# Loading the first four x tiles ahead of the key weights, in smaller pieces on two queues

## The chip, the core and the metric

The kernel runs on one core of a Trainium2 chip. Five engines take part: TensorE (PE; its weight loads are listed as PEld), VectorE (DVE), ScalarE (ACT), GpSimd (POOL) and SyncE (SP), which here does nothing but issue DMAs. ScalarE can issue DMAs too. The time is the device time of one execution in microseconds; several executions are measured and their median is given.

## What is computed

The reference mixes two blocks that read the same x (2048 tokens of 512 features, bf16) with a gate per token:

```python
g = sigmoid((x * gate_w).sum(-1, keepdims=True))
qkv = x @ wqkv                          # 32 heads of 16
pq, pk = phi(q), phi(k)                 # phi(t) = (t + 1 if t > 0 else exp(t)) + 1e-6
kv = einsum("bhsd,bhse->bhde", pk, v);  z = pk summed over s
o  = (pq @ kv) / (pq . z + 1e-6)
a  = o @ wo
b  = (silu(x @ w1) * (x @ w3)) @ w2     # 1376 hidden features
out = g * a + (1 - g) * b
```

## The kernel before, in words

The 2048 tokens are 16 tiles of 128, in four blocks of four tiles. Everything stays on chip: x is held twice, as `x_sb` (tokens on the partitions) and as `xT` (features on the partitions), and so are all weights. The feature dimension of 512 is cut into four chunks, called kc.

The work runs in three stretches. In the first, for each token tile, k is computed by four matmuls (`emit_k_mm`, line 184, one for each kc, with the tile's `xT` as the stationary operand and `wk_sb` as the moving one); ScalarE and VectorE turn it into `pk_sb` (`phi`, lines 138 to 148); GpSimd adds it to a running sum; and four matmuls accumulate XP, the product of x transposed and pk (`emit_xp`, line 204), in the PSUM tiles XP0 to XP3. The second stretch closes the attention state (q of the first block, the remainder columns of the gated block, kvT, W). The third runs through the blocks: gate and up matmuls of the feed-forward part (`emit_ffn`, lines 310 and 318), and output matmuls (`emit_out`, lines 346 to 355), with the q work of the next block between them. The output rows are stored one tile at a time (line 370).

TensorE's order is written out by hand, since its part runs under a manual schedule: it executes the matmuls in the order in which the kernel emits them and waits in that order. The loads are issued on SP's queue in the order in which they are written (lines 83 to 112), except for half of wk, which ScalarE issues at line 84, before its activation table is loaded at line 88. Each load signals its landing on one of eight semaphores that are used in turn, so that in the built program a DMA from the ninth on waits, before it is issued, for the landing of the DMA eight places earlier.

The start is special. The first block's `xT` doesn't come from a transposing load, as that of the other three blocks does (line 90), but from TensorE: `emit_xT(t)` (lines 169 to 181) makes four 128 by 128 transposes of tile t into two PSUM tiles, which VectorE (line 179) and ScalarE (line 181) copy into `xT`. These PSUM tiles are the four buffers of XP0 to XP3, used in turn, and a buffer must have been copied out before its next transpose. Before the first transposes, `emit_warm` runs nine matmuls on constants (line 165) while the first loads are under way. The first x tiles are loaded in pairs: tiles 0 and 1 by one transfer, tiles 2 and 3 by another, where each partition holds two neighbouring rows of the tensor (`x_pairs`, line 81), and the rows of the output are addressed in the same way (`out_pairs`). wk comes in two halves of two kc chunks. So TensorE transposes tiles 0 and 1, computes six k matmuls (kc 0 and 1 for tiles 0 and 1, then kc 2 and 3 for tile 0), transposes tiles 2 and 3, and finishes the other ten k matmuls:

```python
    emit_xT(0)
    emit_xT(1)
    for kc, t in ((0, 0), (1, 0), (0, 1), (1, 1), (2, 0), (3, 0)):
        emit_k_mm(k0[t], t, kc)
    emit_k_phi(k0[0], 0)
    emit_xT(2)
    emit_xT(3)
```

After that, for each tile t from 4 to 15, one XP group (four matmuls) of an earlier tile and the four k matmuls of tile t follow each other.

Of the kernel before, what the change touches and what calls it, by code (L numbers as in the profile page):

```python
# [17 lines left out]
def kernel(  # L18
# [12 lines left out]
    nc = tc.nc  # L31
    P = nc.NUM_PARTITIONS

    Bb, S, D = A_x.shape
# [4 lines left out]
    NT = S // P  # L39
    TB = 512  # L40
    NTB = S // TB
    TPB = TB // P
    FC = F // P
    FR = F - FC * P
    FM = FC * P
# [3 lines left out]
    x2d = A_x.flatten_outer_dims()  # L49
    out2d = out.flatten_outer_dims()  # L50
# [13 lines left out]
    x_sb = consts.tile([P, NT, D], BF16, name="x_sb")  # L64
    xT = consts.tile([P, KC, S], BF16, name="xT")
    wk_sb = consts.tile([P, KC, D], BF16, name="wk_sb")
    wq_sb = consts.tile([P, KC, D], BF16, name="wq_sb")
    wv_sb = consts.tile([P, KC, D], BF16, name="wv_sb")
    w1_sb = consts.tile([P, KC, FM], BF16, name="w1_sb")
    w3_sb = consts.tile([P, KC, FM], BF16, name="w3_sb")  # L70
    wr_sb = consts.tile([P, KC, NR], BF16, name="wr_sb")
    w2_sb = consts.tile([P, FC, D], BF16, name="w2_sb")
# [3 lines left out]
    wqkv_r = A_wqkv.rearrange("(kc d) n -> d kc n", d=P)  # L76
    w1_r = B_w1.rearrange("(kc d) f -> d kc f", d=P)
    w3_r = B_w3.rearrange("(kc d) f -> d kc f", d=P)
    x_r = x2d.rearrange("(t p) d -> p t d", p=P)
    dq = nc.sync  # L80
    x_pairs = x2d[0:TB, :].rearrange("(g p j) d -> g p j d", p=P, j=2)
    out_pairs = out2d[0:TB, :].rearrange("(g p j) d -> g j p d", p=P, j=2)
    dq.dma_start(out=x_sb[:, 0:2, :], in_=x_pairs[0])
    nc.scalar.dma_start(out=wk_sb[:, 0:2, :], in_=wqkv_r[:, 0:2, D : 2 * D])
    dq.dma_start(out=wk_sb[:, 2:4, :], in_=wqkv_r[:, 2:4, D : 2 * D])  # L85
    dq.dma_start(out=x_sb[:, 2:TPB, :], in_=x_pairs[1])
    pre = consts.tile([1, 1], FP32, name="pre")
    nc.scalar.activation(out=pre[:], in_=nc.const_aps.tensor(0.0, [1, 1], FP32), func=ACT.Exp)
    for tb in range(1, NTB):
        dq.dma_start(  # L90
            out=xT[:, :, tb * TB : (tb + 1) * TB], in_=x2d[tb * TB : (tb + 1) * TB, :],
            transpose=True,
        )
        dq.dma_start(
            out=x_sb[:, tb * TPB : (tb + 1) * TPB, :], in_=x_r[:, tb * TPB : (tb + 1) * TPB, :]
        )
    dq.dma_start(out=wq_sb[:], in_=wqkv_r[:, :, 0:D])
    dq.dma_start(out=wr_sb[:, :, 0:FR], in_=w1_r[:, :, FM:F])
    dq.dma_start(out=wr_sb[:, :, FR : 2 * FR], in_=w3_r[:, :, FM:F])
    with nc.allow_non_contiguous_dma(reason="one gate weight per partition and chunk"):  # L100
        dq.dma_start(
            out=wr_sb[:, :, 2 * FR : NR], in_=gate_w.rearrange("(kc d o) -> d kc o", d=P, o=1)
        )
    dq.dma_start(out=wv_sb[:], in_=wqkv_r[:, :, 2 * D : 3 * D])
    for fsl in (slice(0, FM // 2), slice(FM // 2, FM)):
        dq.dma_start(out=w1_sb[:, :, fsl], in_=w1_r[:, :, fsl])
        dq.dma_start(out=w3_sb[:, :, fsl], in_=w3_r[:, :, fsl])
    dq.dma_start(out=wo_sb[:], in_=A_wo.rearrange("(kc d) n -> d kc n", d=P))
    w2_r = B_w2[0:FM, :].rearrange("(fc f) d -> f fc d", f=P)
    for fcs in (slice(0, FC // 2), slice(FC // 2, FC)):  # L110
        dq.dma_start(out=w2_sb[:, fcs, :], in_=w2_r[:, fcs, :])
    dq.dma_start(out=w2r_sb[:FR, :], in_=B_w2[FM:F, :])

    pk_sb = consts.tile([P, NT, D], BF16, name="pk_sb")
# [5 lines left out]
        out=bm, in_=bm, pattern=[[-Dh, HPC], [0, Dh]], compare_op=ALU.is_ge, fill=0.0,  # L120
# [3 lines left out]
        out=bm, in_=bm, pattern=[[Dh, HPC], [0, Dh]], compare_op=ALU.is_ge, fill=0.0,  # L124
# [33 lines left out]
    def emit_warm(*widths):  # L158
        warm = psX.tile([P, TB], FP32, tag="XP3", name="warm")
        for n in widths:  # L160
            nc.tensor.matmul(
                warm[:, 0:n], lhsT=warm_l, rhs=warm_r[:, 0:n], start=True, stop=True
            )

    emit_warm(TB, TB, TB, TB, TB, TB, P, P, P)

    st = {}

    def emit_xT(t):
        for h in range(2):  # L170
            xTp = psX.tile([P, 2, P], BF16, tag=f"XP{(2 * t + h) % 4}", name="xTp")
            for j in range(2):
                kc = 2 * h + j
                nc.tensor.transpose(  # L174
                    out=xTp[:, j, :], in_=x_sb[:, t, kc * P : (kc + 1) * P], identity=ident[:]
                )
            xT_t = xT[:, 2 * h : 2 * h + 2, t * P : (t + 1) * P]
            if h == 0:
                nc.vector.tensor_copy(out=xT_t, in_=xTp[:])
            else:  # L180
                nc.scalar.activation(out=xT_t, in_=xTp[:], func=ACT.Copy)
# [7 lines left out]
    def emit_k_phi(k_ps, t):  # L189
        e_ins = phi(pk_sb[:, t, :], k_ps[:])  # L190
        if t == 0:
            nc.gpsimd.tensor_copy(pks[:], pk_sb[:, t, :])
        else:
            nc.gpsimd.tensor_add(pks[:], pks[:], pk_sb[:, t, :])  # L194
# [137 lines left out]
    def emit_out(tb, tt):  # L332
        t = tb * TPB + tt
        tsl = slice(tt * P, (tt + 1) * P)

        if t < NT - 1:
            parts = [(0, D, True)]
        else:
            h, q3 = D // 2, 3 * D // 4
            parts = [(0, h, True), (h, q3, False), (q3, D, True)]  # L340
        o_out = work.tile([P, D], BF16, tag="o_out", name="o_out")
        lo = 0
        for i, (a, b, store) in enumerate(parts):
            o_ps = psX.tile([P, b - a], FP32, tag=f"XP{2 + (tt + i) % 2}", name="o_ps")
            for c in range(KC):
                nc.tensor.matmul(  # L346
                    o_ps[:], lhsT=st[tb, "pqT"][:, c, tsl], rhs=W_sb[:, c, a:b],
                    start=(c == 0), stop=False,
                )
            nc.tensor.matmul(  # L350
                o_ps[:], lhsT=st[tb, "hTr"][:FR, tsl], rhs=w2r_sb[:FR, a:b],
                start=False, stop=False,
            )
            for fc in range(FC):
                nc.tensor.matmul(  # L355
                    o_ps[:], lhsT=st[tb, "hT"][:, fc, tsl], rhs=w2_sb[:, fc, a:b],
                    start=False, stop=(fc == FC - 1),
                )
            if i < 2:
                nc.scalar.activation(  # L360
                    out=o_out[:, a:b], in_=o_ps[:], func=ACT.Copy, scale=omg[:, t : t + 1]
                )
            else:
                nc.vector.tensor_scalar(
                    out=o_out[:, a:b], in0=o_ps[:], scalar1=omg[:, t : t + 1], scalar2=None,
                    op0=ALU.mult,
                )
            if store:
                rows = out_pairs[t // 2, t % 2] if t < TPB else out2d[t * P : (t + 1) * P, :]
                nc.sync.dma_start(out=rows[:, lo:b], in_=o_out[:, lo:b])  # L370
                lo = b


    k0 = [psM.tile([P, D], FP32, tag="mm", name=f"k0_{t}") for t in range(TPB)]
    emit_xT(0)
    emit_xT(1)
    for kc, t in ((0, 0), (1, 0), (0, 1), (1, 1), (2, 0), (3, 0)):
        emit_k_mm(k0[t], t, kc)
    emit_k_phi(k0[0], 0)
    emit_xT(2)  # L380
    emit_xT(3)
    for t in range(1, TPB):
        for kc in range(2 if t == 1 else 0, KC):
            emit_k_mm(k0[t], t, kc)
# [23 lines left out]
    for c in range(KC):  # L408
# [7 lines left out]
        out=kvT_sb[:], in0=kvT_ps[:],  # L416
# [26 lines left out]
    for tb in range(NTB):  # L443
        for fc in range(FC if tb == 0 else 0, FC):
            emit_ffn(tb, fc)
        nx = tb + 1
        for tt in range(TPB):
            if nx < NTB:
                emit_q(nx, tt, psX, "XP0")
                if tt % 2 == 0:  # L450
                    emit_rem(nx, tt // 2, psX, "XP1")
            emit_out(tb, tt)
            if nx < NTB:
                emit_den(nx, tt)
        if nx < NTB:
            emit_norm(nx)
# [30 lines left out]
```

## Time and profile before

| what | value |
|---|---|
| median of 4 runs | 180.09 us (180.0 to 180.59) |
| the profiled execution's own time | 180.4 us |
| its span, from the first to the last instruction | 178.7 us |
| TensorE matmul busy | 173.5 us, 97% of the span |
| VectorE, ScalarE, GpSimd busy | 118.6, 66.8, 61.4 us |
| bytes read from memory, written | 8.42 MB, 2.10 MB |
| the chain that ended last, by engine | PE 94%, DMA 3%, issue 1% |
| mean granted TensorE clock | 1.00 |

The span leaves out 1.7 us of the profiled execution's time that lie around it. The page also cuts the span into 40 slices of about 4.5 us; the first four engine rows of it give the busy share of each slice in tenths, the last two rows the share of the 16 DMA engines and what they moved:

```profile
PE   7999999999999999999999999999999999999993
DVE  1478867896998837398786375978754669776000
DMA  5999999911006010124000111240001023300011
GB/s 173 234 278 249 263 273 373 347 52 28 9 12 107 0 48 29 44 54 93 0 4 6 38 37 37 59 93 2 0 7 59 15 62 65 60 0 0 29 44 50
```

TensorE is busy in nine tenths of every slice but the first and the last; the DMA engines are busy for the first eight slices, while x and all the weights come in. A busy share says only where an engine works, not what the end waits for; that is what the chain of waits is for, which goes back from the last instruction to whatever released each step. In the timelines below, a row gives the start, the length, the engine, the line and the number of instructions merged into it, and in brackets how long the engine was idle before it and until what.

### The profile page before, as it was taken

What the parts mean: (1) busy time and instruction counts of PE and PEld (TensorE: products, weight loads), DVE (VectorE), ACT (ScalarE), POOL (GpSimd) and SP (SyncE); (2) the same over time, 40 slices, a digit from 0 to 9 for tenths busy, and PEclk for the clock granted to TensorE, in tenths of its full rate; (3) what the DMA queues carried; (4) which work ended last, traced back from release to release, by engine and by line L of the source; (5) the groups of instructions that cost most, each with busy time, mean ns of one, the idle gap of its engine ahead of it and who ended that gap; (6) DMA issues with size and microseconds to landing.
All of it is one profiled execution on the core that took longest, in us unless ns stands there. A gap on an engine that the chain in (4) does not pass through costs nothing.

```text
span 178.7 us, 2472 instructions
## 1 busy us (share of the span) xinstructions
PE 173.5 (97%) x877; PEld 84.1 (47%) x893; DVE 118.6 (66%) x205; ACT 66.8 (37%) x126; POOL 61.4 (34%) x69
## 2 busy tenths in 40 slices
PE   7999999999999999999999999999999999999993
PEld 3444444474444545444444544444545444444463
DVE  1478867896998837398786375978754669776000
ACT  4642323476533333342433333342433323341221
POOL 5186675736353323262003232620032328100000
DMA  5999999911006010124000111240001023300011
GB/s 173 234 278 249 263 273 373 347 52 28 9 12 107 0 48 29 44 54 93 0 4 6 38 37 37 59 93 2 0 7 59 15 62 65 60 0 0 29 44 50
DMA packets 29085, 14.88 MB, mean 83 GB/s; under 512 B 19632, under 2 KB 28816, under 8 KB 29072
## 3 DMA queue, kind: packets, MB, share of 16 engines
q1 hardware_dynamic: 28800, 14.46, 30.6%
q10 hardware_dynamic: 272, 0.26, 0.5%
q8 instruction: 7, 0.11, 0.3%
q14 instruction: 6, 0.05, 0.1%
HBM read 8.42 MB, written 2.10 MB: 59 GB/s over the span
## 4 chain that ended last, share of the span: by engine, by line
PE 94%; DMA 3%; issue 1%; SPq 0%; DVE 0%; DVEq 0%
PE o_ps L355 19%; PE gate_ps L310 19%; PE up_ps L318 19%; PE o_ps L346 8%; PE q_ps L217 8%; PE XP L204 8%; PE k_ps L184 6%; PE r_ps L241 3%; DMA x_sb<-in_A_x_dram 3%; PE o_ps L350 2%; PE k L184 1%; PE kvT_ps L411 0%; PE W_ps L438 0%; PE xTp L174 0%; SPq L85 0%
## 5 line engine op out<-in xcount | busy, mean ns | idle before, releaser
L310 PE MATMUL gate_ps<-xT,w_sb 128*128 128x512 bf16 x156 | 40.7, 379 | 0.2
L318 PE MATMUL up_ps<-xT,w_sb 128*128 128x512 bf16 x156 | 40.5, 379 | 0.2
L225 POOL TENSOR_TENSOR qz<-pq,z_sb 128x512 f32<-128x512 bf16 x16 | 18.5, 1164 | 60.3 <-DVE pq L145 58.4
L323 ACT ACTIVATE th<-gate_ps 128x512 bf16<-128x512 f32 x40 | 23.9, 597 | 38.1 <-PE gate_ps L310 36.6
L355 PE MATMUL o_ps<-w_sb,hT 128*128 128x512 bf16 (+2 forms) x176 | 37.3, 354 | 0.2
L325 DVE SCALAR_TENSOR_TENSOR gs<-th,gate_ps 128x512 bf16<-128x512 bf16 x40 | 27.3, 683 | 5.8 <-ACT th L323 5.6
L328 DVE TENSOR_TENSOR hT<-up_ps,gs 128x512 bf16<-128x512 f32 x40 | 27.6, 691 | 3.8
L142 DVE TENSOR_SCALAR phi_m<-phi_e 128x512 bf16<-128x512 bf16 x32 | 14.3, 447 | 19.5 <-ACT phi_e L140 19.4
L355 PEld LDWEIGHTS <-hT 128*128 128x128 bf16 x180 | 16.8, 97 | 17.9
L318 PEld LDWEIGHTS <-w_sb 128*128 128x128 bf16 x160 | 15.6, 98 | 18.9
L310 PEld LDWEIGHTS <-w_sb 128*128 128x128 bf16 x160 | 15.6, 98 | 18.6
L360 ACT ACTIVATE o_out<-o_ps,omg 128x512 bf16<-128x512 f32 (+2 forms) x17 | 11.2, 656 | 30.4 <-PE o_ps L355 30.4
L290 POOL TENSOR_TENSOR pqn<-pq,rden 128x512 bf16<-128x512 bf16 x16 | 16.6, 1058 | 14.0 <-DVE rden L283 11.7
L194 POOL TENSOR_TENSOR pks<-pks,pk_sb 128x512 f32<-128x512 f32 x15 | 17.4, 1163 | 8.1 <-DVE pk_sb L145 7.5
L228 DVE TENSOR_REDUCE den<-qz 128x32 f32<-128x512 f32 x16 | 11.0, 684 | 9.0 <-POOL qz L225 8.9
L346 PE MATMUL o_ps<-W_sb,pqT 128*128 128x512 bf16 (+2 forms) x71 | 16.5, 355 | 0.1
L217 PE MATMUL q_ps<-wq_sb,xT 128*128 128x512 bf16 x63 | 16.4, 379 | 0.1
L204 PE MATMUL XP<-pk_sb,x_sb 128*128 128x512 bf16 x62 | 16.0, 379 | 0.1
L140 ACT ACTIVATE phi_e<-k_ps 128x512 bf16<-128x512 f32 x12 | 7.2, 598 | 14.4 <-PE k_ps L184 14.4
L140 ACT ACTIVATE phi_e<-q_ps 128x512 bf16<-128x512 f32 x16 | 9.6, 597 | 7.8 <-PE q_ps L217 7.8
L184 PE MATMUL k_ps<-wk_sb,xT 128*128 128x512 bf16 x48 | 12.3, 379 | 0.1
L145 DVE SCALAR_TENSOR_TENSOR pq<-q_ps,phi_m 128x512 bf16<-128x512 f32 x16 | 11.1, 691 | 0.5
(59 smaller groups left out, 117.6 us busy)
## 6 DMA issues: line engine op xcount, KB each, us to landing
w_sb<-in_B_w_dram SPq DMA_DIRECT2D x6, 640.0 KB, 9.2
out_dram<-o_out SPq DMA_DIRECT2D x15, 128.0 KB, 1.7
x_sb<-in_A_x_dram SPq DMA_DIRECT2D x3, 512.0 KB, 4.3
x_sb<-in_A_x_dram SPq DMA_DIRECT2D x2, 256.0 KB, 3.7
wq_sb<-in_A_wqkv_dram SPq DMA_DIRECT2D x1, 512.0 KB, 6.1
wv_sb<-in_A_wqkv_dram SPq DMA_DIRECT2D x1, 512.0 KB, 6.2
wo_sb<-in_A_wo_dram SPq DMA_DIRECT2D x1, 512.0 KB, 10.6
wk_sb<-in_A_wqkv_dram ACTq DMA_DIRECT2D x1, 256.0 KB, 3.8
```

What stands on the lines that cost most here:

```text
L184: nc.tensor.matmul(k_ps[:], lhsT=xT[:, kc, t * P : (t + 1) * P], rhs=wk_sb[:, kc, :], start=(kc == 0), stop=(kc == KC - 1),)
L194: nc.gpsimd.tensor_add(pks[:], pks[:], pk_sb[:, t, :])
L204: nc.tensor.matmul(XP_ps[dc][:], lhsT=x_sb[:, t, dc * P : (dc + 1) * P], rhs=pk_sb[:, t, :], start=(t == 0), stop=(t == NT - 1),)
L217: nc.tensor.matmul(q_ps[:], lhsT=xT[:, kc, ts_tok], rhs=wq_sb[:, kc, :], start=(kc == 0), stop=(kc == KC - 1),)
L225: nc.gpsimd.tensor_tensor(out=qz[:], in0=st[tb, "pq"][:, tt, :], in1=z_sb[:], op=ALU.mult)
L310: nc.tensor.matmul(gate_ps[:], lhsT=w1_sb[:, kc, fsl], rhs=xT[:, kc, tok_sl], start=(kc == 0), stop=(kc == KC - 1),)
L318: nc.tensor.matmul(up_ps[:], lhsT=w3_sb[:, kc, fsl], rhs=xT[:, kc, tok_sl], start=(kc == 0), stop=(kc == KC - 1),)
L323: nc.scalar.activation(out=th[:], in_=gate_ps[:], func=ACT.Tanh, scale=0.5)
L325: nc.vector.scalar_tensor_tensor(out=gs[:], in0=th[:], scalar=1.0, in1=gate_ps[:], op0=ALU.add, op1=ALU.mult)
L328: nc.vector.tensor_tensor(out=st[tb, "hT"][:, fc, :], in0=up_ps[:], in1=gs[:], op=ALU.mult)
L346: nc.tensor.matmul(o_ps[:], lhsT=st[tb, "pqT"][:, c, tsl], rhs=W_sb[:, c, a:b], start=(c == 0), stop=False,)
L355: nc.tensor.matmul(o_ps[:], lhsT=st[tb, "hT"][:, fc, tsl], rhs=w2_sb[:, fc, a:b], start=False, stop=(fc == FC - 1),)
```

## The change

The first eight loads are one x tile or one kc chunk of wk each, 128 KB, instead of four loads of 256 KB. The four x tiles go first, alternating between SP's queue and ScalarE's; of the wk chunks ScalarE issues the second, SP the others. Partitions hold single rows again, so the output rows of the first block are addressed like the others. All 16 transposes stand before the first k matmul, and the order of the k matmuls among themselves is as it was. There is one 512-wide warm matmul less. Further back in SP's queue, the x tiles of blocks 2 and 3 come in one load, which stands before the last transposing load instead of partly behind it, and w1, w3 and w2 are each loaded whole instead of in halves.

```diff
-    x_pairs = x2d[0:TB, :].rearrange("(g p j) d -> g p j d", p=P, j=2)
-    out_pairs = out2d[0:TB, :].rearrange("(g p j) d -> g j p d", p=P, j=2)
-    dq.dma_start(out=x_sb[:, 0:2, :], in_=x_pairs[0])
-    nc.scalar.dma_start(out=wk_sb[:, 0:2, :], in_=wqkv_r[:, 0:2, D : 2 * D])
-    dq.dma_start(out=wk_sb[:, 2:4, :], in_=wqkv_r[:, 2:4, D : 2 * D])
-    dq.dma_start(out=x_sb[:, 2:TPB, :], in_=x_pairs[1])
+    aq = nc.scalar
+    for q, t in ((dq, 0), (aq, 1), (dq, 2), (aq, 3)):
+        q.dma_start(out=x_sb[:, t, :], in_=x_r[:, t, :])
+    for q, kc in ((dq, 0), (aq, 1), (dq, 2), (dq, 3)):
+        q.dma_start(out=wk_sb[:, kc, :], in_=wqkv_r[:, kc, D : 2 * D])
...
-        dq.dma_start(
-            out=x_sb[:, tb * TPB : (tb + 1) * TPB, :], in_=x_r[:, tb * TPB : (tb + 1) * TPB, :]
-        )
+        if tb < NTB - 1:
+            x_ts = slice(tb * TPB, (tb + 1) * TPB if tb < NTB - 2 else NT)
+            dq.dma_start(out=x_sb[:, x_ts, :], in_=x_r[:, x_ts, :])
...
-    for fsl in (slice(0, FM // 2), slice(FM // 2, FM)):
-        dq.dma_start(out=w1_sb[:, :, fsl], in_=w1_r[:, :, fsl])
-        dq.dma_start(out=w3_sb[:, :, fsl], in_=w3_r[:, :, fsl])
+    dq.dma_start(out=w1_sb[:], in_=w1_r[:, :, 0:FM])
+    dq.dma_start(out=w3_sb[:], in_=w3_r[:, :, 0:FM])
...
-    w2_r = B_w2[0:FM, :].rearrange("(fc f) d -> f fc d", f=P)
-    for fcs in (slice(0, FC // 2), slice(FC // 2, FC)):
-        dq.dma_start(out=w2_sb[:, fcs, :], in_=w2_r[:, fcs, :])
+    dq.dma_start(out=w2_sb[:], in_=B_w2[0:FM, :].rearrange("(fc f) d -> f fc d", f=P))
...
-    emit_warm(TB, TB, TB, TB, TB, TB, P, P, P)
+    emit_warm(TB, TB, TB, TB, TB, P, P, P)
...
-                rows = out_pairs[t // 2, t % 2] if t < TPB else out2d[t * P : (t + 1) * P, :]
-                nc.sync.dma_start(out=rows[:, lo:b], in_=o_out[:, lo:b])
+                nc.sync.dma_start(
+                    out=out2d[t * P : (t + 1) * P, lo:b], in_=o_out[:, lo:b]
+                )
...
-    emit_xT(0)
-    emit_xT(1)
+    for t in range(TPB):
+        emit_xT(t)
     for kc, t in ((0, 0), (1, 0), (0, 1), (1, 1), (2, 0), (3, 0)):
         emit_k_mm(k0[t], t, kc)
     emit_k_phi(k0[0], 0)
-    emit_xT(2)
-    emit_xT(3)
```

## The prediction

> **What bounds the kernel now.** I read the page's busy shares first (PE 97%), then the chain of waits, to see whether anything but PE sets the end, then TensorE's timeline in the first 10 us, since the change touches almost nothing else. The chain at the start (start us, length us, what):
>
> ```profile
> 1.72 4.60 DMA x_sb<-in_A_x_dram
> 6.32 0.05 issue
> 6.37 0.62 PE xTp L174 x8
> 6.99 2.16 PE k L184 x10
> 9.15 0.86 PE XP L204 x4
> ```
>
> The end hangs on one transfer, the second pair of x tiles: issued at 1.72, landed at 6.32. After it come eight transposes and ten k matmuls; the first XP starts at 9.15. From there on TensorE has next to no gaps (columns: length, PE, PEld, DVE, ACT, POOL busy, clock, DMA share, GB/s):
>
> ```profile
> 9.15:36.60 27.45, 27.29 (x125) 12.43 (x127) 21.43 (x35) 10.48 (x18) 19.21 (x17) 1.00 1.03 295
> 36.60:175.90 139.30, 138.51 (x712) 68.03 (x723) 93.75 (x162) 51.69 (x100) 39.13 (x40) 1.00 0.14 35
> ```
>
> So what the change does to the start of the first XP it does to the end, unless a later transfer becomes late. Everything below is a sum over 0 to 9.15. TensorE's timeline there (start, length, line, count, idle before):
>
> ```profile
> 3.35 0.39 PE L161 MATMUL warm<-const-bfloat16-1.0 128*128 128x128 bf16 x3
> 3.67 0.62 PE L174 MATMUL xTp<-ident,x_sb 128*128 128x128 bf16 x8
> 4.64 1.46 PE L184 MATMUL k<-wk_sb,xT 128*128 128x512 bf16 x6 [0.36 <-DMA wk_sb<-in_A_wqkv_dram]
> 6.37 0.62 PE L174 MATMUL xTp<-ident,x_sb 128*128 128x128 bf16 x8 [0.27 <-DMA x_sb<-in_A_x_dram]
> ```
>
> The pace is read from it: a transpose every 0.62/8 = 0.078 us, a k matmul every 2.16/10 = 0.216. Real work before 9.15 is 16 x 0.078 + 16 x 0.216 = 4.7 us; it began at 3.67, so 0.8 us are waits. They are what can be won, plus an earlier beginning.
>
> **When the bytes come.** Both versions load the same 1024 KB first, so the byte rate of before, in half microseconds, is my lower bound (GB/s is the last column; 74 in the half before 2.00):
>
> ```profile
> 2.00:2.50 0.50, 0.50 (x2) 0.15 (x1) 0.00 (x0) 0.50 (x1) 0.50 (x3) 1.00 0.83 197
> 2.50:3.00 0.50, 0.50 (x3) 0.22 (x2) 0.00 (x0) 0.26 (x2) 0.50 (x2) 1.00 0.89 311
> 3.00:3.50 0.50, 0.50 (x4) 0.22 (x3) 0.00 (x0) 0.00 (x0) 0.00 (x0) 1.00 1.09 322
> 3.50:4.00 0.50, 0.50 (x10) 0.41 (x9) 0.01 (x1) 0.00 (x0) 0.00 (x0) 1.00 0.96 279
> 4.00:4.50 0.50, 0.28 (x6) 0.20 (x3) 0.50 (x2) 0.40 (x2) 0.00 (x0) 1.00 1.13 389
> 4.50:5.00 0.50, 0.36 (x2) 0.19 (x2) 0.00 (x1) 0.26 (x1) 0.00 (x0) 1.00 1.05 388
> ```
>
> Summed, 256 KB have moved at 2.9, 512 at 3.8, 768 at 4.5, 1024 at 5.2. The upper bound is when whole transfers of that sum had landed, by issue plus time to landing:
>
> ```profile
> x_sb<-in_A_x_dram SPq DMA_DIRECT2D x1, 256.0 KB, 2.8
> wk_sb<-in_A_wqkv_dram ACTq DMA_DIRECT2D x1, 256.0 KB, 3.8
> wk_sb<-in_A_wqkv_dram SPq DMA_DIRECT2D x1, 256.0 KB, 4.0
> x_sb<-in_A_x_dram SPq DMA_DIRECT2D x1, 256.0 KB, 4.6
> xT<-in_A_x_dram SPq DMA_TRANSPOSE x1, 5.9
> ```
>
> 0.80 + 2.8 = 3.6, 0.80 + 3.8 = 4.6, 1.26 + 4.0 = 5.26, 1.72 + 4.6 = 6.32.
>
> **Part by part.** *Loads.* Issues stand 0.46 us apart on a queue (0.80, 1.26, 1.72). After: SP issues x0 at 0.80, x2 1.26, wk0 1.72, wk2 2.18, wk3 2.64; ACT issues x1 at 0.80, x3 1.26, wk1 1.72. The trace has no 128 KB load, so between the bounds I take the middle: x0 and x1 land at 3.25 (2.9 to 3.6), x2 and x3 at 4.2 (3.8 to 4.6), wk0 and wk1 at 4.9 (4.5 to 5.26). For wk3, the last, the ends are 5.2 (bytes) and 2.64 + 4.6 = 7.24 (the slowest time to landing from its later issue). The nearest row is 6.32, the same 1024 KB, then with the transposing load of xT right behind from 2.23; that starts 0.9 later now, so I take 6.1.
>
> *Warm matmuls.* One 512-wide one less, 0.43 us at the cold pace (weight loads at 1.22, 1.65, 2.08), so the warm run ends at 3.3 rather than about 3.7. x0 lands then (3.25), so nothing waits there.
>
> *ScalarE.* Two more DMA issues stand before its table load, 2 x 0.46. Its row before:
>
> ```profile
> 1.27 1.28 ACT L88 ACT_TABLE_LOAD   x1 [1.27 <-PEq L471]
> 2.57 0.20 ACT L88 ACTIVATE pre<-const-float32-0.0 1x1 f32<-1x1 f32 x1
> 4.10 0.66 ACT L181 ACTIVATE xT<-xTp 128x256 bf16<-128x256 bf16 x2 [1.33 <-PE xTp L174]
> ```
>
> The 1.33 us of idle before the first copy hides the 0.92, but hardly more: ACT is free at 3.7 and its first copy is due at about 3.7. Without that cover each microsecond of ACT delay would go onto the transposes.
>
> *Transposes.* All 16 share four PSUM buffers, so those of x2 and x3 now wait for the copies of x0 and x1: two DVE copies take 0.52, two on ACT 0.66. ACT's first two end at 3.8 + 0.66 = 4.5, DVE's earlier; with x2 and x3 landed at 4.2 the last transpose ends at about 4.5 + 0.3 = 4.85. The copies' new wait thus costs no more than about 0.1.
>
> *k matmuls.* They start at 4.9 with wk0; five (kc 0, 1 for two tiles, then kc 2) take 1.08, to 5.98; the sixth needs wk3 at 6.1; it and the ten behind it take 11 x 0.216 = 2.38, end 8.48. The first XP also needs pk of tile 0: last k matmul at 6.1 + 0.38, exponential 0.60, two DVE steps 0.28 + 0.69, with gaps about 8.1. So XP starts at **8.48 instead of 9.15: 0.67 us won.**
>
> *What is late next: xT of the second block.* The two built programs' orders show that each load waits for the landing of the one eight places earlier. Ninth was the third transposing load; ninth now is the first, behind x0. It cannot issue before 0.80 + 5 x 0.46 = 3.1, and x0 lands at 3.25; plus 5.9 that is 9.15. The fifth k tile needs it at 8.48 + 0.86 = 9.34: covered by 0.2 us. With x0 at 3.6 it is 9.5, which costs 0.16. Behind it on SP everything moves by about 1 us: xT of block 2 lands near 13.5 and is due near 16.
>
> *Merged x, w1, w3 and w2 loads.* Four SP issues fewer than split ones, no fewer bytes. The last half of w3 landed at 22.35 + 9.2 = 31.6 and the first gate matmul starts at 38.9; wholes landing even 3 us later stay hidden, since PE's 27.45 us stretch covers them. The x of blocks 2 and 3, now in one 1 MB load issued near 11.4 and due at about 22, is hidden too. The out rows change only addresses. All this: 0, up to +0.2.
>
> Sum: the profiled execution, 180.4 (span 178.7), becomes 179.7. The median of the runs is 180.09, 0.3 below that execution, so I forecast 180.09 - 0.67 = **179.4**.
>
> [...] The trace shows the clock opening inside the warm run: the narrow warm matmuls take 281 ns first and 243 on average over three, so it switched near 3.45, 2.6 us after the first matmul. After the change the warm run ends at 3.3 and transposes follow. [...] By the row the missing 0.15 us is a trifle[...], sum -0.67. [...]
>
> **The rivals.** *The last wk piece is late.* For it: eight transfers instead of four, and last in line took 4.0 to 4.6 from issue. At 4.0 wk3 lands at 6.64, XP starts at 9.02: 179.96; at 4.6 9.62: 180.56. Against: the bytes are the same and the later issues leave the queues shorter. I put it at **180.0**; it loses from a wk3 landing past 6.77.
>
> [...] The place is the 16 k matmuls. [...] **181.15**. It decides against the change from three slow k matmuls on. Against it: [...] before's four runs lie within 0.6 us.
>
> *That the change doesn't do what it says* is out: in the built order all 16 transposes stand before the k matmuls.
>
> **How the numbers follow.** Forecast 0.50 (own range 179.1 to 179.75), late wk 0.28, clock 0.22. A measurement of this kernel tells 0.3% (0.54 us) from no change, so faster means under 179.55. Faster: 0.38 of the first and 0.05 of the second, 0.43. Same: 0.12, 0.17, 0.06 = 0.35. Slower: 0.06 and 0.16, 0.22. The range 179.1 to 180.9 leaves out a little below and the upper half of the clock case.
>
> **What would show it.** Right: transposes starting at 3.3, k matmuls at 4.9 at 0.216 each, XP at 8.3 to 8.7, no new TensorE gap after. Wrong: k matmuls 0.43 apart past 5 us; an idle of over 0.5 before the sixth; a wait for xT at the fifth tile; an ACT copy starting past 4.3; any wait for w1 or w3 near 39.

## The result, and the profile after

The changed kernel takes a median of 180.85 us (180.18 to 183.0, 39 runs) against 180.25 us (179.93 to 181.11, 58 runs) for the one before on the same chip: a ratio of 1.0038, interval 1.0025 to 1.0051. It is slower by about 0.6 us, a little more than the 0.3% that a measurement can tell. Forecast was a gain of 0.67 us. The profiled execution after took 181.19 us (span 179.5), the one before 180.4 (span 178.7).

The chain of waits at the start, after (start, length, what):

```profile
1.73 3.81 DMA wk_sb<-in_A_wqkv_dram
5.58 4.35 PE k L180 x16
9.93 0.86 PE XP L200 x4
```

The chain no longer hangs on x but on a piece of wk, and the first XP starts at 9.93 instead of 9.15: 0.78 us later, which is the whole difference of the two spans. From there on TensorE has no new gap (174.7 us busy, 97% of the span). In every trace of this study but two the execution's time less the start of the first XP is 171.23 to 171.29 us: 180.4 - 9.15 before, 181.19 - 9.93 after. So all of the question lies in the first 10 us, and an execution without a trace still tells when its first XP began: the median after at 180.85 - 171.25 = 9.6, the median before at 9.0.

TensorE's timeline after, the transposes:

```profile
3.62 1.89 PE L170 MATMUL xTp<-ident,x_sb 128*128 128x128 bf16 x16 [0.17 <-DMA x_sb<-in_A_x_dram]
```

They begin at 3.62 and end at 5.51. The weight loads (PEld), one for each transpose, show the pace better than such a row, whose length has the tail of its last matmul in it. The first eight before, then the sixteen after:

```profile
3.66 0.45 PEld L174 LDWEIGHTS <-x_sb 128*128 128x128 bf16 x8
3.62 1.63 PEld L170 LDWEIGHTS <-x_sb 128*128 128x128 bf16 x16 [0.44 <-DMA x_sb<-in_A_x_dram]
```

That is 0.45/8 = 0.056 us for a transpose before and 1.63/16 = 0.102 after. The weight loads of the k matmuls after (one row for those that follow each other closely):

```profile
6.39 0.15 PEld L180 LDWEIGHTS <-xT 128*128 128x128 bf16 x1 [0.28 <-issue]
6.81 0.15 PEld L180 LDWEIGHTS <-xT 128*128 128x128 bf16 x1 [0.27 <-issue]
7.18 2.26 PEld L180 LDWEIGHTS <-xT 128*128 128x128 bf16 x11 [0.21 <-issue]
```

The first two stand 0.42 us apart, the next 0.37, and from then on it is 2.26/11 = 0.21: TensorE ran at half pace until about 7.1 us, in before's profiled execution until about 3.5. Below, "the clock opens" means this doubling of the pace. The profile's own column of the granted clock reads 1.00 in both stretches, so the moment is read from the distance between matmuls, or worked out from how long a row of them took. And the landings of the first eight loads after (queue, size, us from issue to landing):

```profile
x_sb<-in_A_x_dram SPq DMA_DIRECT2D x2, 128.0 KB, 2.8
x_sb<-in_A_x_dram ACTq DMA_DIRECT2D x2, 128.0 KB, 3.0
wk_sb<-in_A_wqkv_dram SPq DMA_DIRECT2D x3, 128.0 KB, 3.8
wk_sb<-in_A_wqkv_dram ACTq DMA_DIRECT2D x1, 128.0 KB, 4.0
```

The first x tile, 128 KB, took 2.8 us, as long as the 256 KB of before. The wk pieces issued at 1.73 landed at 5.54 and 5.73. So two things end at the same moment, the sixteenth transpose at 5.51 and the first piece of wk at 5.54.

### The profile page after: what moved, and what is told of

The parts are those of the page before. It is cut to its first block, busy times and chain, and to the rows that moved or that the text cites. A ratio compares the mean times of both kernels' runs of the same rounds, so it can differ in the third digit from the quotient of the medians.

```text
span 179.5 us, 2470 instructions
## 1 busy us (share of the span) xinstructions
PE 174.7 (97%) x876; PEld 85.0 (47%) x892; DVE 118.0 (66%) x205; ACT 66.9 (37%) x126; POOL 61.3 (34%) x69
## 4 chain that ended last, share of the span: by engine, by line
PE 95%; DMA 2%; issue 1%; SPq 0%; DVE 0%; DVEq 0%
PE o_ps L351 19%; PE gate_ps L306 19%; PE up_ps L314 19%; PE o_ps L342 8%; PE q_ps L213 8%; PE XP L200 8%; PE k_ps L180 6%; PE r_ps L237 3%; PE k L180 2%; DMA wk_sb<-in_A_wqkv_dram 2%; PE o_ps L346 2%; PE kvT_ps L406 0%; PE W_ps L433 0%; SPq L83 0%; DVE o_out L360 0%
## 5 line engine op out<-in xcount | busy, mean ns | idle before, releaser
L138 DVE TENSOR_SCALAR phi_m<-phi_e 128x512 bf16<-128x512 bf16 x32 | 13.7, 427 | 22.3 <-ACT phi_e L136 22.2
```

## The experiments

The theories: **pieces** (eight loads land later than four, and k waits for wk), **clock** (it opens late, so that transposes and the first k matmuls run at half pace), **missing warm matmul** (why the clock is late), **merged loads** (the loads further back cost something). Below, "six warms" means the six 512-wide matmuls of before in place of five. Each result stands beside runs of the kernel before on the same chip (medians 180.30 to 180.38).

### The warm matmuls

a_warm6, the changed kernel with six warms:

```diff
-    emit_warm(TB, TB, TB, TB, TB, P, P, P)
+    emit_warm(TB, TB, TB, TB, TB, TB, P, P, P)
```

> The changed kernel with the sixth wide warm matmul back, nothing else. Theory: [...] the k matmuls run 0.216 apart from the start, XP starts at 5.58 + 3.46 = 9.05 to 9.1, and the median falls by about 0.8, to 180.1. [...] the k matmuls stay slow in part and the median falls by 0.4 at most. Rival: the loss is the late landing of the first wk piece (5.53) alone: no change, 180.85.

Measured: 180.84 us (180.36 to 181.35, 22 runs) beside 180.35, ratio 1.0021 (1.0012 to 1.0029). Its chain:

```profile
3.88 1.29 PE xTp L170 x14
...
5.47 3.60 PE k L180 x16
9.07 0.86 PE XP L200 x4
```

This execution, at 180.36 the fastest of its runs, is what the theory expected: the clock opened among the transposes, by 4.9 at the latest (an estimate: the fourteen in 1.29 us are ten at 0.106 us, the 0.85/8 of w_order2's at half pace, and four at 0.056), and XP starts at 9.07. The first wk piece came early (4.8) and k waited for the transposes; the k matmuls stand 0.216 us apart, with 0.15 more before the sixth, whose wk piece, the last, landed at 6.5. But the median lost as much as without the sixth warm matmul, but one thing differs: of the 39 runs of the changed kernel six lie at 182.67 to 183.0 and none between 181.35 and 182.67; here none lies above 181.35.

b_warm5, the kernel before with five warms (the same line, one TB less):

> The kernel before with five wide warm matmuls instead of six, nothing else: the one removed matmul by itself. [...] the warm run ends at 3.3, the x tiles land at 3.6, [...] six k matmuls run at half pace between 4.64 and 7.0, which the wait for the second x pair (6.32) hides in part: median 180.3 to 180.9, more spread. Rival: the warm matmul doesn't matter, since the span was bound by the x pair at 6.32: 180.1 to 180.3.

Measured: 180.49 us (22 runs, 180.09 to 181.39 and one at 182.8), ratio 1.0008 (0.9996 to 1.0021). Its trace is of a late clock (opened near 6.5): the first eight transposes take 1.03 us, from 4.06, the six k matmuls behind them 2.02, XP starts at 9.72. The median can't be told from that of six warms.

a_warm3, the changed kernel with three 512-wide warm matmuls, shows the late opening enlarged:

```diff
-    emit_warm(TB, TB, TB, TB, TB, P, P, P)
+    emit_warm(TB, TB, TB, P, P, P)
```

> The changed kernel with three wide warm matmuls instead of five. Theory: the executions 2 us above the rest[...]: with the warm run ending at 2.4 [...] the median is 181.8 to 182.8, and the trace shows ten or more k matmuls 0.43 apart. Rival: that group has nothing to do with the warm run: the median stays at 180.9 to 181.2.

Measured: 181.92 us (181.0 to 182.82, 6 runs), ratio 1.0084 (1.0053 to 1.0115). Its weight loads of k stand 0.43 us apart up to these two rows, and 1.61/8 = 0.20 in the second:

```profile
8.36 0.15 PEld L180 LDWEIGHTS <-xT 128*128 128x128 bf16 x1 [0.27 <-issue]
8.78 1.61 PEld L180 LDWEIGHTS <-xT 128*128 128x128 bf16 x8 [0.27 <-issue]
```

The half pace lasts to about 8.8; the sixteen k matmuls take 5.04 us instead of 3.45, and XP starts at 10.89 (182.15 us). A run at 182.8 would have its XP at 182.8 - 171.25 = 11.55. With k from 5.58 on and 0.43 and 0.216 us for a matmul, that is an opening near 10.6, an estimate. Such runs came in kernels with five or three wide warms, and in none of the 21 to 28 runs each of a_warm6, a_fill, b_tail, b_k7q and w_order with w_order2, all with six, nor in any run of the kernel before (181.11 at most). That the six slow runs of the changed kernel are of this kind is inferred from their size; none of them was traced.

a_fill adds matmuls on constants between the transposes (into a bank that the k matmuls overwrite), so that TensorE works without a pause from 0.84 us on:

```diff
-    for t in range(TPB):
+    for t, n in zip(range(TPB), (256, 256, 256, TB)):
         emit_xT(t)
+        emit_fill(n)
```

> The changed kernel with the sixth warm matmul and with one matmul on constants behind each tile's transposes (256, 256, 256 and 512 wide), which do no work of the kernel. [...] all k matmuls stand 0.216 apart, XP starts near 9.05, the median is 180.0 to 180.2 and the runs at 182.7 to 183 are gone. Rival, late loads alone: the fillers add up to 0.5 us of work in front of the k matmuls but inside the wait for wk, so 180.85 to 181.2.

Measured: 180.86 us (180.51 to 181.46, 21 runs), ratio 1.0029 (1.002 to 1.0038). In its trace the clock opened only past 5.8 all the same (each four transposes took 0.43 us, the last four, from 5.80, took 0.30), k started at 6.31 and took 3.45, XP 9.77. This trace shows no earlier opening, and the fillers used up the time they were to win.

### The loads further back

b_tail, the kernel before with only the merged later loads of the change (x of blocks 2 and 3, w1, w3, w2):

```diff
+        if tb < NTB - 1:
+            x_ts = slice(tb * TPB, (tb + 1) * TPB if tb < NTB - 2 else NT)
+            dq.dma_start(out=x_sb[:, x_ts, :], in_=x_r[:, x_ts, :])
...
+    dq.dma_start(out=w1_sb[:], in_=w1_r[:, :, 0:FM])
+    dq.dma_start(out=w3_sb[:], in_=w3_r[:, :, 0:FM])
```

> The kernel before with the later loads merged as in the change (x of blocks 2 and 3 in one load, w1, w3 and w2 whole), nothing else. Both theories: no difference, 180.0 to 180.3. If the merged loads cost anything, it shows as a gap of TensorE near 22 or near 39.

Measured: 180.69 us (180.29 to 181.43, 22 runs), ratio 1.0013 (1.0002 to 1.0024). XP starts at 9.14, as before, and nothing is late between: the last VectorE instruction ends at the same 175.89. What is longer is the very end, where SP waits for the last store. The waits of SP on that store, first in b_tail:

```profile
SPq L479 <- DMA out_dram<-o_out: 1.2, 1, 1.2
```

and in b_lane, the same kernel with wq loaded in four pieces and wv in two, so that the last store again signals on the semaphore it has in the kernel before:

```profile
SPq L483 <- DMA out_dram<-o_out: 0.9, 1, 0.9
```

```diff
-    dq.dma_start(out=wq_sb[:], in_=wqkv_r[:, :, 0:D])
+    for kc in range(KC):
+        dq.dma_start(out=wq_sb[:, kc, :], in_=wqkv_r[:, kc, 0:D])
```

> b_tail with four loads more (wq in four pieces, wv in two), which come long before they are needed. In b_tail the number of DMAs is four smaller than before, so that the last output store signals on another of the eight semaphores, and the wait behind it took 1.2 us instead of 0.9. Theory that the final waits stand in the order of these semaphores: with four loads more the last store is back on the old one, the wait is 0.9 again and the median is that of before, 180.25 to 180.4. Rival, merged loads cost something themselves: 180.6 to 180.7 as in b_tail.

Measured: 180.44 us (179.88 to 181.07, 14 runs) beside 180.38, ratio 1.0004 (0.9992 to 1.0016). So merging the loads costs nothing where they are used. In the changed kernel the last wait is 0.9 as well; its loss isn't here.

### Pieces apart from the clock

To hold the clock still, the loads are put behind a delay during which TensorE is kept busy. In the first pair, b_open and a_open, twenty warm matmuls made the delay:

```diff
+    warm0 = emit_warm(psX, "XP3", *([TB] * 20))
+    for sb in (x_sb[:, 0:TPB, 0:2], wk_sb[:, :, 0:2]):
+        nc.vector.tensor_copy(out=sb, in_=warm0[:, 0:8].rearrange("p (a b) -> p a b", b=2))
```

> The kernel before [...] 20 wide matmuls on constants run first, and no load may be issued until they are done (small copies of their result into the loads' destinations hold the loads back); then 14 more warm matmuls stand where the warm run stood. All instructions of the kernel follow as before, some 9 us later. Both theories: the k matmuls run 0.216 apart in every execution. [...] This is the base for a_open.

> The changed kernel with [...] in the same way. Theory A, the loss is the clock: [...] the k matmuls start when the first wk piece lands (4.7 us after the first load's issue) and take 3.46 us, so that XP starts 8.2 to 8.3 us after the first issue, as in the kernel before (8.35): a_open is within 0.2 us of b_open. Theory B, the loss is the loads' arrival: a_open stays 0.4 to 0.7 us above b_open, as without the warm start.

Measured: 187.5 us (186.46 to 187.74, 5 runs) and 187.29 (186.57 to 188.01, 6 runs). This settled nothing: the delay is made of matmuls, and so depends on when the clock opens (20 took 5.87 us in the trace). From the first issue to XP the traces show 15.18 - 6.93 = 8.25 and 15.32 - 6.91 = 8.41.

In the second pair, b_fix and a_fix, twelve VectorE reductions (0.70 us each in both traces) make the delay, while matmuls fill most of TensorE's time up to the landing of x:

```diff
+    emit_warm(psX, "XP3", *([TB] * 28))
+    for i in range(12):
+        nc.vector.tensor_reduce(
+            out=hold[:], in_=dummy[:].rearrange("p (a b) -> p a b", b=TB // 8),
+            axis=AX.X, op=ALU.add,
+        )
```

> The kernel before behind a fixed delay: VectorE runs twelve reductions on constants (0.68 us each) before any load may be issued, while TensorE runs 28 wide warm matmuls, [...] 10 more warm matmuls stand where the warm run stood. Base for a_fix. Both theories: all k matmuls 0.216 apart[...].

> The changed kernel behind the same fixed delay, clock open. In b_open and a_open XP started 8.25 and 8.41 after the first load's issue, but the medians could not tell (the delay itself depended on the clock). Theory A, the loss is the clock alone: a_fix within 0.1 us of b_fix. Theory B, it is the loads alone: a_fix 0.5 to 0.7 above b_fix. Theory C, both: the loads cost 0.15 to 0.35 (k matmuls start at 4.73 after the first issue and take 3.46, 8.2 to 8.4, against 7.85 to 8.35 for before), the clock the rest.

Measured: b_fix 190.03 us (189.91 to 190.22, 4 runs), a_fix 190.55 (190.22 to 190.79, and one run at 192.39, 6 runs). Both issue their first load at 10.63, and behind it their k matmuls run at the open clock (ten in 2.16 us in b_fix, 0.216 each, and all sixteen in 3.61 in a_fix, against 4.35 after). The chain of b_fix:

```profile
11.55 4.28 DMA x_sb<-in_A_x_dram
...
18.66 0.86 PE XP L229 x4
```

and TensorE's timeline of a_fix:

```profile
13.51 1.40 PE L195 MATMUL xTp<-ident,x_sb 128*128 128x128 bf16 x16 [0.57 <-DMA x_sb<-in_A_x_dram]
15.54 3.61 PE L205 MATMUL k<-wk_sb,xT 128*128 128x512 bf16 x15 [0.62 <-DMA wk_sb<-in_A_wqkv_dram]
```

With the clock out of the way the change still costs 190.55 - 190.03 = 0.52 us. Transposes are done at 14.91, and TensorE then waits 0.62 us for the first piece of wk. XP starts at 19.15 instead of 18.66. The four runs of b_fix lie within 0.3 us, the 58 of the kernel before within 1.2 (four drawn from these lie within 0.6 on average). How much of that scatter is the clock's opening isn't shown, since behind the delay the loads start 10 us later too, and without it the second x pair landed anywhere from 5.78 (b_lane) to 6.62 (b_k7). The run at 192.39 has no trace; it stays unexplained.

c_fix is a_fix with the same order (x first, then wk, all transposes first) in four loads of 256 KB:

```diff
+    dq.dma_start(out=x_sb[:, 0:2, :], in_=x_pairs[0])
+    aq.dma_start(out=x_sb[:, 2:TPB, :], in_=x_pairs[1])
+    dq.dma_start(out=wk_sb[:, 0:2, :], in_=wqkv_r[:, 0:2, D : 2 * D])
+    dq.dma_start(out=wk_sb[:, 2:4, :], in_=wqkv_r[:, 2:4, D : 2 * D])
```

> a_fix with the first 1024 KB in four loads of 256 KB, in the new order (x pair 0 on SP, x pair 1 on ScalarE's queue, both wk halves on SP); wq and wv are split so that the last store signals on the same semaphore. Theory, the order costs: the first wk half lands 4.7 to 4.9 after the first issue, median 190.35 to 190.55 as a_fix. Rival, the pieces cost: it lands by 4.4, median 190.0 to 190.15 as b_fix.

Measured: 190.18 us (190.13 to 190.23, 5 runs), 0.15 behind b_fix and 0.37 ahead of a_fix. (c_fix and w_fix ran on another chip than these two; the kernel before took 180.34 there and 180.35 here.) Its chain has no wait for wk:

```profile
15.41 3.45 PE k L212 x16
18.86 0.86 PE XP L232 x4
```

The first half of wk landed at 14.80, 0.7 us before the first piece in a_fix; 0.46 of that is its place in SP's queue, second instead of third. The first x, a pair now, landed later than the single tile of a_fix, at 13.87 instead of 13.37.

w_fix keeps the pieces and the fixed delay but goes back to the old order, x0 and x1, wk, then x2 and x3, with the transposes in two groups:

```diff
-    for q, t in ((dq, 0), (aq, 1), (dq, 2), (aq, 3)):
+    for q, t in ((dq, 0), (aq, 1)):
...
+    for q, t in ((dq, 2), (dq, 3)):
+        q.dma_start(out=x_sb[:, t, :], in_=x_r[:, t, :])
```

> a_fix with the order of before in 128 KB pieces: x0 and x1, then the four wk pieces, then x2 and x3, and TensorE's order of before (transposes of tiles 2 and 3 behind six k matmuls). Theory, the order costs the 0.5 us (wk behind all of x, so that TensorE idles between transposes and k): the first k matmul starts about 4.0 after the first load's issue as in b_fix instead of 4.9, XP at 8.0 to 8.1, median within 0.15 of b_fix (190.0). Rival, the pieces cost it: wk pieces and the last x tiles land late here too, median 190.4 to 190.6 as a_fix.

Measured: 190.62 us (190.51 to 190.78, 5 runs), 0.59 behind b_fix. In TensorE's timeline the fifth k matmul waits for the later pieces of wk:

```profile
16.06 0.59 PE L207 MATMUL k<-wk_sb,xT 128*128 128x512 bf16 x2 [0.87 <-DMA wk_sb<-in_A_wqkv_dram]
```

So it is the pieces that cost half a microsecond at an open clock, in either order. The order alone costs 0.15, which four and five runs with overlapping ranges hardly tell from nothing. Whether pieces cost by their number on a queue or by their smaller size no run separates.

### Pieces taken away at the clock as it is

c_pairs6 is the changed kernel with six warms and the four loads of c_fix, without the delay:

> The changed kernel with six wide warm matmuls and with its first eight loads of 128 KB put back into four of 256 KB in the new order: x tiles 0 and 1 on SP, 2 and 3 on ScalarE's queue, then both halves of wk on SP. Theory that eight pieces land late because there are eight (issues and 1 KB rows): the first wk half lands by 4.9 to 5.2, the k matmuls start then, 0.4 earlier than with pieces, and the median is 0.2 to 0.4 below a_warm6, 180.4 to 180.6. Rival, the order alone decides (wk behind all of x): wk lands at 5.4 or later as with pieces, and the median is that of a_warm6, 180.7 to 180.9.

Measured: 180.91 us (180.67 to 181.56, 13 runs) beside 180.38, ratio 1.003 (1.0018 to 1.0041). The first half of wk landed at 4.96, as expected, but k waited for the transposes until 5.95, and the median is above the expectation. Here, as in b_tail, the last wait is 1.2 us. c_lane, the same with wq and wv split as in b_lane, has the last store on its old semaphore:

> c_pairs6 with wq in four loads and wv in two, so that the last store signals on the same semaphore as in before and after. c_fix stood 0.15 above b_fix and 0.37 below a_fix. If that holds without the delay, the median is 0.1 to 0.3 above before, 180.5 to 180.65, and 0.26 below that of c_pairs6 (180.91).

Measured: 180.84 us (180.39 to 181.21, 13 runs) beside 180.30, ratio 1.0028 (1.0014 to 1.0043). That is above the expectation: the last wait went back to 0.9 in the trace, and the median hardly moved. Its chain:

```profile
0.80 3.34 DMA x_sb<-in_A_x_dram
...
4.18 1.89 PE xTp L176 x16
6.08 3.50 PE k L186 x16
```

The first half of wk is there at 5.2; the transposes alone hold k back to 6.08. They take 1.89 us, as in the changed kernel (the clock opened near 6.1: the k matmuls behind them took 3.50, 0.05 more than at the open clock), and start from an x pair that landed at 4.14, where the single tile landed at 3.58.

The runs together, as loss against their own baseline (medians, us; six warms or an open clock, so the missing warm matmul is in none):

| | x and wk in eight 128 KB pieces | in four 256 KB loads |
|---|---|---|
| clock as it comes | +0.49 (a_warm6) | +0.54 (c_lane) |
| clock held open | +0.52 (a_fix) | +0.15 (c_fix) |

Neither cure alone helps; both together win most of it back, though the second row rests on four to six runs each. With pieces, k waits for wk, and slow transposes end at about the same time. With 256 KB loads wk is early, but the first x comes half a microsecond later, and from there the transposes take 1.89 us at half pace and 1.40 (14.01 to 15.41) at the open clock. So each cure alone uncovers the other wait.

### Versions that might be faster

w_order, without delay: six warms, pieces, the old order of loads and transposes (the diff of w_fix without the delay); w_order2 repeats it with more rounds.

> The changed kernel with six wide warm matmuls, its 128 KB pieces in the order x0, x1, wk, x2, x3, and TensorE's order of before. Theory that the order is the cause: median 180.2 to 180.4, that of before; lower if the halved pieces let the first k matmul start sooner. Rival, the pieces are the cause: 180.7 to 180.9, as a_warm6.

> w_order once more, unchanged, for more executions beside kernels of one session. If pieces cost in the old order too, as w_fix says, the median is 0.3 to 0.6 above that of before; if only the new order makes them costly, within 0.15 of before.

Measured: 180.52 us (180.03 to 180.71, 6 runs), ratio 1.0 (0.9979 to 1.0021), then 180.59 (179.81 to 181.09, 22 runs), ratio 1.0016 (1.0005 to 1.0028). Better than the changed kernel, not better than before. It should lose as much as w_fix, and lost less; its landings differ between executions (the median wk piece of a queue landed 3.1 and 3.4 us after its issue in the first trace, 3.6 and 3.9 in the second), and this isn't settled. One part can be read from the second trace: the last two wk pieces landed at 6.15 and 6.40, as late after the first issue as in w_fix, but the four k matmuls ahead of them ran at half pace until 6.24, so that TensorE lost next to nothing by waiting. The clock of this one kernel opened near 4.9 in the first trace and near 6.7 in the second, where the first six k matmuls took 1.44 and 2.32 us.

b_k7, the kernel before with a seventh k matmul ahead of the second transposes, and b_k7q, where ScalarE also issues the second x pair:

```diff
-    for kc, t in ((0, 0), (1, 0), (0, 1), (1, 1), (2, 0), (3, 0)):
+    for kc, t in ((0, 0), (1, 0), (0, 1), (1, 1), (2, 0), (3, 0), (2, 1)):
```

> The kernel before with seven instead of six k matmuls ahead of the second transposes (kc 2 of tile 1 moves up); nothing else. Theory that TensorE's wait for the second x pair and its slow clock both sit here: where the pair lands late, the moved matmul fills 0.2 us of the wait, and where it lands early it costs nothing: median 0.05 to 0.2 below before, 180.15 to 180.3. Rival: the copies of the later transposes then come too late, so the gain is lost: 180.35 or more.

> b_k7 with the load of the second x pair issued by ScalarE, at 1.26 instead of SP's 1.72; it delays ScalarE's table load by 0.46, which its idle time covers. Theory that a queue's earlier issue brings the bytes earlier: the pair lands by 0.2 to 0.4 sooner, median 0.1 to 0.2 below b_k7. Rival: the DMA engines share the same bytes, so the pair lands sooner only by delaying the wk halves: no gain, or 0.1 slower.

Measured: 180.37 us (14 runs), ratio 0.9994 (0.9979 to 1.001), and 180.6 (22 runs), ratio 1.0012 (1.0002 to 1.0021). No gain is shown by the first, and the second is slower. No version beat both kernels.

## Why the prediction was wrong

**The bound was right.** Time hangs on the start of the first XP, and everything behind it stayed hidden: ScalarE's table load (2.21 to 3.49) ended before the first copy at 4.27; xT of the second block landed at 3.77 + 5.0 = 8.77, in time; the merged loads cost nothing. So the sum over the first 10 us was the right sum.

**The step that failed** is "The trace has no 128 KB load, so between the bounds I take the middle". For the landings the lower bound was a count of bytes, and half of that count went into the forecast. But time to landing hardly shrank with size: x0 took 2.8 us at 128 KB as at 256, so it came at 3.6 (3.25 forecast, and 3.6 was the upper bound). wk0 came at 5.54 and wk1 at 5.73 (4.9 forecast, upper bound 5.26, so outside it): they are third on their queues, issued 0.93 us after the first, and took 3.8 and 4.0 from there, as the 256 KB halves had. In a_warm3 wk0 came later still (5.81); only a_warm6's trace has it where it was forecast. The upper bound of 5.26 was the old issue time, 1.26, plus the old 4.0, although the same part lists the new issue at 1.72; 1.72 + 4.0 is what was measured. a_fix against c_fix shows what it is worth by itself: 0.37 us. In this execution it alone takes most of the win: k at 5.58 and 3.45 us at the open clock would put XP at 9.03, an estimate, 0.12 ahead of before instead of 0.67. wk3 came at 6.7, 0.6 later than forecast, and cost nothing here, because by then the k matmuls were slow and late; in a_warm6's trace it cost 0.15.

**The second step that failed** is the pace: a transpose every 0.078 and a k matmul every 0.216, "read from" the profiled execution as if fixed. That execution had its clock open near 3.5, as early as any trace here (b_tail's is the same); in the other traces with five or six wide warms it opened between 4.6 (b_lane) and 7.1 (after). In the kernel before this matters less, because the slow part (eight transposes, six k matmuls) lies partly in the wait for the second x pair (b_warm5, with its clock open near 6.5, started XP at 9.72). The change puts all 16 transposes on the path ahead of k: 1.89 us instead of the 16 x 0.078 = 1.25 of that pace, from 3.62 instead of 3.3, which ends them at 5.51 instead of 4.85. Two readings in that sum are off as well. The 0.62 us for eight transposes has the tail of the last in it; they start 0.056 apart. And the copies' wait, put at no more than 0.1, is about 0.34 where the clock is open: in a_fix the sixteen take 1.40, and without waits it would be 15 x 0.056 + 0.22 = 1.06, an estimate (0.22 for the whole of the last). At half pace no such wait shows: the sixteen stand 0.102 us apart, no more than the 0.106 of w_order2's first eight, which need no buffer back. k starts at 5.58 instead of 4.9, and takes 4.35 instead of 3.58: 0.68 + 0.77 = 1.45, which is 9.93 against the 8.48 of the sum.

**The rivals.** The clock rival, at 181.15, named what this execution shows: k matmuls 0.43 apart past 5 us, here until about 7.1. It was too high for the median; that it was off by only 0.3 is in part luck: above the forecast of 179.4 it allowed 1.75 us for slow k matmuls, and they cost 0.77 here (4.35 instead of 3.58), but its sum kept the landings and the transposes as forecast, and both were slower: the errors partly cancel. The late-wk rival was right in kind but named the wrong piece: wk0, not wk3. Weighing a late opening against the one row of before was right: the opening moved from 3.5 to 7.1 us among the traces with five or six wide warms. When it would come was the author's estimate, and what sets that moment no run here shows.

**The warm run** ended at 3.45 (3.3 forecast), and the missing 0.15 us of busy time, called a trifle, was not one: it goes with the runs near 182.8. Six of 39 runs that are 2.0 us longer raise the mean by 0.3 us, and the mean loss is 181.08 - 180.35 = 0.73; the other 0.42 are late pieces and slow transposes. The first is inferred from which kernels had such runs; for the second, the table above shows a loss of that size without the missing matmul.

Open are the run of a_fix at 192.39, why w_order loses less than w_fix over all its runs, and why pieces land as late as loads of twice their size.

## What to carry to other kernels

Time to landing at the start of this kernel hardly depended on the size: the first x load on SP took 2.6 to 2.8 us in pieces of 128 KB and 2.7 to 3.3 in pairs of 256 KB. Cutting a load in two gives two issues (0.46 us apart on a queue here), and what stands behind lands later (the first wk, by 0.7 us in a_fix against c_fix), so put what is needed first in few loads, and count the place in its queue for each. Don't take the pace of the first microseconds from one execution (TensorE's doubled anywhere from 3.5 to 7.1 us here): read it from several, and ask which part of the slow stretch is hidden behind a load; work that is moved from behind such a wait onto the path is paid at the slow pace (sixteen transposes: 1.89 us instead of 1.40). When two things end at the same time, undoing either may show nothing: undo both.

## What was not expected of the hardware

The clock opened at very different times under nearly the same load of TensorE: about 3.5 us (before, b_tail), 4.6 (b_lane), 4.9 at the latest (a_warm6), past 5.8 (a_fill, where TensorE never paused from 0.84 on), 6.5 (b_warm5), 7.1 (after), and 8.8 with three wide warms (a_warm3). The same kernel had 4.9 in one execution and 6.7 in another (w_order, w_order2). Transposes follow the clock like matmuls: 0.056 us apart where it is open (before, 0.45/8), 0.102 where it isn't (after, 1.63/16), as k matmuls stand 0.216 and 0.43 apart.

The wait behind the last store (64 KB, half of the last tile) is 0.9 us or 1.2 us, and goes with which of the eight semaphores it signals: 1.2 in b_tail and c_pairs6, 0.9 in every other trace, also where splitting wq and wv put it back. In b_tail and c_pairs6 the time less the start of XP is 171.51 instead of 171.25. The medians follow it in b_lane (180.44 for 180.69) and hardly in c_lane (180.84 for 180.91).
